# One kernel of attention and two mixtures on one core: another order of the head, value products by 128 rows, another end of the running sums

## The chip, the cores and the metric

The kernel runs on one core of a Trainium2 chip. The metric is the time of one execution on the device in microseconds (us). The engines are TensorE (PE), VectorE (DVE), ScalarE (ACT), GpSimd (POOL) and SyncE (SP), which here only starts transfers. Each works through its own instructions in the order in which the program writes them, and waits where data or a buffer isn't ready. The kernel before takes 391.78 us, the median of three runs.

## The reference, cut to what matters

Three stages follow each other: masked attention over 4 batches of 576 tokens with 8 heads of 64 (heads 0 to 3 see a window of 32 tokens, heads 4 to 7 every 32nd token), a feed-forward block with a squared relu, and a soft mixture of experts with 8 experts of 4 slots.

```python
scores = scale * np.matmul(q, k.transpose(0, 1, 3, 2))
scores = np.where(masks[None], scores, -1e9); scores -= scores.max(-1, keepdims=True)
attn = np.exp(scores); attn /= attn.sum(-1, keepdims=True) + 1e-9
x = (attn @ v).transpose(0, 2, 1, 3).reshape(2304, 512)
...
h = x @ w_in                       # 512 -> 2048
g = np.maximum(h, 0) ** 2
x = g @ w_out                      # 2048 -> 512
...
logits = x @ phi                   # 32 slots
d = np.exp(logits - logits.max(0)); d /= d.sum(0) + 1e-9
slot_input = d.T @ x               # 8 experts x 4 slots
h = np.maximum(slot_input[e] @ w1[e], 0)          # 512 -> 1024
slot_out[e] = h @ w2[e]                           # 1024 -> 512
c = np.exp(logits - logits.max(1, keepdims=True)); c /= c.sum(1, keepdims=True) + 1e-9
out = c @ slot_out
```

## The kernel before, in words

Tokens are cut into five blocks (512, 512, 512, 512, 256). For each block there are 16 product steps, 80 in all: step s multiplies x, transposed, by 128 columns of `w_in` (`gemm1`, L474). x and `w_in` are both kept as a high and a low part, so one step is 12 products. ACT takes the relu out of PSUM (L493), ACT or POOL squares it (L497, L499), and DVE transposes it to tokens (L506). The second matrix is never applied to tokens. `matrix` (L535 to L547) multiplies `w_out` by phi, `logits` (L527) takes the slots' logits from the squared steps, and `Dispatch` keeps a running maximum over tokens (`nm_run`) and running sums: `total` makes logits by slot and the maximum (L569 to L575), `turn` the rescaling factor `al` and the turned weights, and `slots` (L598) is the group-summing product, which sums the squared steps by slot into two PSUM tiles `four`. For blocks 0 to 2 the sums of earlier blocks are kept elsewhere and added; from block 3 on (`KEEP`) `scale` (L590 on ACT, L591 on DVE) rescales `four` in place and `slots` adds to it. In the last block `last_step` (L513 to L515), `last_turn` (L616 to L622) and `last_sums` (L628 copies, L632 products, L633 transposes) do the same, and `hold` (L874) issues dummy products. After that come the slots' inputs (L896 and on), the experts (L935, L962) and the output (L980).

Attention is cut into 16 units, one for each batch and pair of heads; pairs 0 and 1 are local, pairs 2 and 3 strided. For the first eight units PE writes the mask (L247) and the scores (L258), DVE takes the negative row maxima (L262), PE subtracts them (`less`, L268), and ACT takes the exponential (L274). DVE sums (L319) and inverts (L322 to L325), POOL or DVE scales (L328), and PE turns the weights into the PSUM tile `turned` (L342), from which ACT or DVE moves them to `ptl` or `pts` (L353); later units turn on DVE (L363). The value products (L391) write two tiles, `oa` and `ob`. The high part of x is a cast (L406), the low part a subtraction on DVE (L407).

The weights' bits arrive as raw words (L424, SP) and are put together before use: ACT brings the upper word into range (L442), DVE shifts (L445) and joins the lower word (L449); for `w_in` a cast to the high part (L454, on ACT, POOL or DVE) and the low part (L458, on DVE or POOL) follow. Conversions 0 to 7 are `w_in` (tiles `y`), from 8 on the other matrix (tiles `wo`).

What sets the order: everything up to product step 18 stands in a hand-written string `HEAD`, whose tokens are issued one after the other: `A3` is the next step of unit 3, `C2` the next step of conversion 2, `G4` a quarter of product step 4, `R`, `X`, `T` its relu, square and transpose, `P` a step of `matrix`, `L` logits, `q`, `v`, `l`, `f` loads, `w9` nine dummy products (L742). A letter A, D or P at the end names the engine. Later work hangs on positions, four for each step (`at(position, function)`), which run between the quarters of a product step. So an engine's order is that of the tokens that use it.

The functions are printed here with the line numbers that the profile uses.

## Time and profile before

| | |
|---|---|
| median of three runs | 391.78 us (391.52 to 394.02) |
| profiled execution, its own time | 393.14 us |
| its span, first to last instruction | 391.3 us |
| mean granted clock of TensorE | 0.992 |
| busy: PE / DVE / ACT / POOL | 368.7 / 246.1 / 176.7 / 55.5 us |
| HBM read | 75.25 MB, 204 GB/s over the span with what is written |

A row of the timeline gives the start of an instruction (or of several alike in sequence, with their count), its duration, the engine, the line and the tiles, and in brackets the idle time of that engine just before it with what ended that. A product in fp32 leaves two or more records, so counts of records on PE are not counts of products. A row of the stretches gives each engine's busy time between two points of the span, then PE's granted clock as a share of 2.4 GHz, the transfers' share and their rate.

### The profile page before, as it was taken

Reading aid. Unit: us, or ns where it says so; the run is one execution under the profiler, and the core shown is the slowest. Engines: PE = TensorE matmul, PEld = TensorE weight load, DVE = VectorE, ACT = ScalarE, POOL = GpSimd, SP = SyncE. Lnnn points to the kernel's source line nnn. Section 1 sums busy time; section 2 is a strip of 40 time slices with the busy share of each in tenths; the row PEclk is TensorE's granted clock in tenths of the full one; section 3 lists DMA queues with packets and bytes.
Section 4 is the critical chain, followed back from the end, with each engine's and each line's share of the span. In section 5 each row is a group of like instructions: output and inputs, shape, how many; then the busy total and the mean of one; then the engine's idle time right before and its main releaser. Section 6 shows DMA issues by size and latency. Waiting matters only on the chain.

```text
span 391.3 us, 9218 instructions
## 1 busy us (share of the span) xinstructions
PE 368.7 (94%) x3822; PEld 261.7 (67%) x3822; DVE 246.1 (63%) x519; ACT 176.7 (45%) x377; POOL 55.5 (14%) x87
## 2 busy tenths in 40 slices
...
GB/s 243 365 156 396 216 299 309 105 107 243 176 37 92 278 3 75 190 116 123 85 52 78 125 55 219 265 56 162 109 54 151 410 407 381 302 379 411 409 360 239
DMA packets 25353, 80.56 MB, mean 206 GB/s; under 512 B 3040, under 2 KB 3296, under 8 KB 25312
## 3 DMA queue, kind: packets, MB, share of 16 engines
...
q14 instruction: 11, 0.09, 0.1%
HBM read 75.25 MB, written 4.72 MB: 204 GB/s over the span
## 4 chain that ended last, share of the span: by engine, by line
PE 80%; DVE 6%; ACT 3%; issue 2%; DVEq 0%; ACTq 0%
PE h L474 50%; PE four L598 5%; PE so L962 4%; PE eh L935 4%; PE four L527 3%; PE oa L391 3%; PE lg L527 2%; PE out L980 1%; PE ob L391 1%; PE si L896 1%; DVE wo L449 1%; PE lr L569 1%; DVE y L449 1%; PE qa L288 1%; PE pp L535 1%
## 5 line engine op out<-in xcount | busy, mean ns | idle before, releaser
L474 PE MATMUL h<-x,w 128*128 128x512 f32 x768 | 191.6, 400 | 3.2 <-DVE x L407 1.2
L474 PEld LDWEIGHTS h<-x,w 128*128 128x128 f32 x768 | 140.5, 188 | 52.0 <-issue 17.4
L493 ACT ACTIVATE gk<-h 128x512 f32<-128x512 f32 (+1 forms) x70 | 38.4, 550 | 93.8 <-PE h L474 88.0
L506 DVE STREAM_TRANSPOSE gt<-gk 128x512 f32<-128x512 f32 (+1 forms) x71 | 44.4, 641 | 46.5 <-ACT gk L497 40.7
L497 ACT ACTIVATE gk<-gk 128x512 f32<-128x512 f32 (+1 forms) x66 | 38.3, 583 | 1.4
L474 PEld LDWEIGHTS h<-xl,w 128*128 128x128 f32 x192 | 23.6, 191 | 3.5 <-issue 3.4
L474 PE MATMUL h<-xl,w 128*128 128x256 f32 x192 | 25.0, 287 | 0.0
L363 DVE STREAM_TRANSPOSE ptl<-sl 32x320 f32<-32x320 f32 (+1 forms) x48 | 23.7, 493 | 0.7
L449 DVE SCALAR_TENSOR_TENSOR wo<-raw,wo 128x512 uint32<-128x512 uint32 x32 | 23.0, 737 | 0.3
L442 ACT ACTIVATE wo<-raw 128x512 f32<-128x512 f32 x32 | 20.8, 667 | 4.9 <-DMA raw<-woutt 3.6
L598 PE MATMUL four<-gt,lsb 32*32 32x512 f32 x576 | 21.4, 598 | 0.7 <-ACT four L590 0.7
L458 POOL TENSOR_TENSOR w<-y,w 128x512 fp32r<-128x512 f32 x10 | 13.2, 1330 | 34.7 <-ACT w L454 34.7
L598 PEld LDWEIGHTS four<-gt,lsb 32*32 32x32 f32 x576 | 10.0, 103 | 9.2 <-issue 3.5
L407 DVE TENSOR_TENSOR x<-oa,x 128x512 fp32r<-128x512 f32 (+1 forms) x16 | 10.5, 657 | 8.1 <-ACT x L406 5.6
L962 PE MATMUL so<-e,gk 128*32 128x128 f32 (+1 forms) x304 | 14.7, 302 | 0.0
L935 PE MATMUL eh<-e,lsb 128*32 128x512 f32 x104 | 14.3, 594 | 0.4 <-DVE lsb L913 0.4
L406 ACT CAST x<-oa 128x512 fp32r<-128x512 f32 (+1 forms) x16 | 9.6, 598 | 11.0 <-PE oa L391 10.8
L363 DVE STREAM_TRANSPOSE pts<-sw 32x512 f32<-32x512 f32 x20 | 14.0, 700 | 0.6 <-POOL sw L328 0.3
L445 DVE TENSOR_SCALAR wo<-wo 128x1024 uint32<-128x1024 uint32 x16 | 12.4, 777 | 2.3 <-ACT wo L442 2.3
L962 PEld LDWEIGHTS so<-e,gk 128*32 128x32 f32 x304 | 11.1, 110 | 2.4 <-issue 0.8
L799 POOL COPY lsb<-pt 128x128 f32<-128x128 f32 x1 | 0.3, 290 | 85.0 <-PE four L598 85.0
L454 ACT CAST w<-y 128x512 fp32r<-128x512 f32 x15 | 9.1, 617 | 5.7 <-DVE y L449 5.6
...
## 6 DMA issues: line engine op xcount, KB each, us to landing
...
```

Source lines behind the costliest of these rows:

```text
L363: yield "T", lambda e, d=dst, s_=src: DVE.transpose(out=d, in_=s_)
L391: PE.matmul(o[bank][64 * h:64 * h + 64, col:col + w1_ - w0], u.v[0:k, t, 64 * h:64 * h + 64], rhs, start=start, stop=stop, skip_group_chec ...
L442: ACT.activation(y[0][:, z], raws[2 * m + z][:, :, 1].bitcast(F32), AF.Prelu, scale=2.0 ** -112, alpha=2.0 ** 32)
L449: DVE.scalar_tensor_tensor(out=yb, in0=raws[2 * m + z][:, :, 0], scalar=29, in1=yb, op0=ALU.logical_shift_right, op1=ALU.bitwise_or)
L474: PE.matmul(hs[s][0][:, 0:TB[b]], w_in[s % SB][:, a, 128 * kc:128 * kc + 128], x_of(b, kc)[:, x, :] if b < 4 else xl[:, :, kc, x, :], star ...
L493: ACT.activation(gs[s], h[:, 0:TB[s // SB]], AF.Relu)
L497: ACT.activation(gs[s], gs[s], AF.Square)
L506: DVE.transpose(out=by_tokens(b)[:, :, f, :] if b else gt_[0].rearrange("p (f t) -> p f t", f=SB)[:, f], in_=gs[s])
L527: PE.matmul(lg_of(b)[q(y), 0:TB[b]], pt[:, f, :], gs[SB * b + f], start=ch == 0, stop=ch == 3, skip_group_check=True)
L598: PE.matmul(four_[a // 2][q(c % 4), a % 2, :], ext[q(a), c, :], g[q(a), c] if self.b else g[q(a), :, 32 * c:32 * c + 32], start=c < 4 and ...
L935: PE.matmul(hps[g][n][q(j), :], siT[:, kc, :], cols(et[0, g, j, kc], 512 * n, 512), start=kc == 0, stop=kc == 3, skip_group_check=True)
L962: PE.matmul(sums[n][q(j)], hT[g][fc // 4][:, fc % 4, q(j)], cols(et[1 + n, g, j, wd * fc // 1024], wd * fc % 1024, wd), start=g == 0 and f ...
```

## The change

There are three parts. First, `HEAD` is another string of the same 520 steps: the same work in another order, with other engine letters at some steps. On DVE there are fewer moves L353 (5 for 16) and, in exchange, 5 casts L406 and 2 casts L454; on ACT 35 moves L353 for 24, 43 casts L406 for 48 and 5 casts L454 for 15; on POOL 9 casts L454 for 1 (whole program). The nine dummies come first. Second, the last fifth of a local unit's keys (64 of them) is multiplied by all 128 rows of the tiles; the other rows hold zeros. Third, in the last block the running maximum is brought into the maximum's tile by a product with the identity, so that one reduction gives the new one; the running sums are copied to SBUF eight and six positions before the last product step ends, `slots` starts from zero, and eight products with `tal`, the identity times the rescaling factor, add the old sums in `last_sums`.

Of `HEAD`, the first line of each string is shown.

```diff
--- before.py
+++ after.py
@@ -26,6 +26,8 @@
 NSTEP = SB * NBLK
 NG = 7
 NX = 14
+OLD = 1536
+OLD_AT = (8, 6)
 NEG = -1e30
 HEAD_ROW = [0, 1, 0, 1]
 UNITS = [(1, 2), (1, 0), (1, 3), (1, 1), (2, 0), (2, 2), (2, 1), (2, 3), (3, 0), (3, 2), (3, 1), (3, 3)]
@@ -35,22 +37,22 @@
 RAW_AT = [0, 1, 2, 3, 4, 6, 0, 1, 2, 0, 1, 2, 0, 1, 2, 0]
 Y_AT = [2, 0, 0, 1, 1, 3, 3, 2]
 HEAD = """
-A2P A0 A0 A0D w9 q2 A0P A0 A0 A0P A0A A0D A2P A2 A1D w6 A0P l0 C0 l10 l1 C0 C0 C0 A2P A2D A2 A2 A2P C0 f l2 l3 q1 A1P
...
+w9 A0 A0 A0D A0P A0 A0 A0P A0A A2P q2 A2P A2 A0D w6 l2 C1 l3 C1 C1 A2P A2D A2 A2 A0P A0A A0A A0A A0A A0A A0A C1D q1
...
 """
 FILL = 6
 HEAD_STEPS = 18
@@ -65,7 +67,7 @@
 LATE_TZ = 26
 LATE_LZ = 37
 EPS = 1e-9
-HOLD = [5, 1, 0]
+HOLD = [5, 0, 0]
 KEEP = 3
 
 C_ML, C_MS, C_ID, C_TI, C_RM, C_LO, C_END = 0, 128, 146, 274, 402, 403, 404
@@ -128,6 +130,7 @@
         tiny = cp.tile([128, 104], F32, name="tiny")
         ident = c[:, C_ID:C_ID + 128]
         tident = c[:, C_TI:C_TI + 128]
+        tal = cp.tile([128, NS], F32, name="tal")
         xr = {}
 
         def ring(n, z, shape, dt, name):
@@ -375,10 +378,10 @@
                 if self.local:
                     plan = []
                     for t in range(5):
-                        k, x0, x1 = (64, 512, 576) if t == 4 else (128, 128 * t, 128 * t + 160)
+                        x0, x1 = (512, 576) if t == 4 else (128 * t, 128 * t + 160)
                         for bank, y0, y1 in ((0, x0, min(x1, 512)), (1, max(x0, 512), x1)):
                             if y0 < y1:
-                                plan.append((t, k, y0 - x0, y1 - x0, bank, y0 - 512 * bank, t == 3 * bank, t == 3 + bank))
+                                plan.append((t, 128, y0 - x0, y1 - x0, bank, y0 - 512 * bank, t == 3 * bank, t == 3 + bank))
                 else:
                     plan = [(t, 128, 0, 72, t // 4, 72 * (t % 4), True, True) for t in range(8)]
 
@@ -566,12 +569,15 @@
             def total(self):
                 o = self.o = ps("at", f"lr{self.b}")
                 T = self.T
+                if self.b == NBLK - 1:
+                    PE.matmul(o[:, T:T + 1], ident, bm, start=True, stop=True)
                 PE.matmul(o[:, 0:T], tident, lsb[:, 0:T], start=True, stop=self.b < NBLK - 1)
                 if self.b == NBLK - 1:
                     PE.matmul(o[:, 0:T], lsb[:, 384:512], gs[NSTEP - 1], start=False, stop=True)
-                DVE.tensor_reduce(out=bm, in_=o[:, 0:T], op=ALU.max, axis=AX.X, negate=True)
-                DVE.tensor_tensor(out=nm, in0=bm, in1=nm_run, op=ALU.min)
-                if self.b < NBLK - 1:
+                    DVE.tensor_reduce(out=nm, in_=o[:, 0:T + 1], op=ALU.max, axis=AX.X, negate=True)
+                else:
+                    DVE.tensor_reduce(out=bm, in_=o[:, 0:T], op=ALU.max, axis=AX.X, negate=True)
+                    DVE.tensor_tensor(out=nm, in0=bm, in1=nm_run, op=ALU.min)
                     ACT.activation(lg_of(self.b)[:, 0:T], o[:, 0:T], AF.Exp, bias=nm, accum_out=bs)
 
             def turn(self):
@@ -582,6 +588,8 @@
                 DVE.transpose(out=lsb[:, 0:T], in_=lg_of(self.b)[:, 0:T])
                 ACT.activation(al, nm_run, AF.Exp, scale=-1.0, bias=nm)
                 DVE.tensor_copy(nm_run, nm)
+                if self.b == NBLK - 2:
+                    DVE.tensor_scalar_mul(bm, nm, -1.0)
                 if self.b >= KEEP:
                     self.scale()
 
@@ -597,7 +605,7 @@
                     for a in range(4):
                         PE.matmul(four_[a // 2][q(c % 4), a % 2, :], ext[q(a), c, :],
                                   g[q(a), c] if self.b else g[q(a), :, 32 * c:32 * c + 32],
-                                  start=c < 4 and self.b < KEEP, stop=c >= num - 4, skip_group_check=True)
+                                  start=c < 4 and (self.b < KEEP or self.b == NBLK - 1), stop=c >= num - 4, skip_group_check=True)
 
             def sums(self):
                 for n in range(2):
@@ -611,25 +619,32 @@
 
             def last_turn(self):
                 z = [slice(0, 128), slice(128, 256)]
-                e_ = gk_[0][:, 2560:2816]
+                e_ = gk_[0][:, 0:256]
                 for n in range(2):
                     ACT.activation(e_[:, z[n]], self.o[:, z[n]], AF.Exp, bias=nm, accum_out=(bs, bs2)[n])
                     DVE.transpose(out=lsb[:, z[n]], in_=e_[:, z[n]])
                 ACT.activation(al, nm_run, AF.Exp, scale=-1.0, bias=nm)
-                self.scale()
+                DVE.tensor_scalar_mul(tal, tident[:, 0:NS], al)
                 ov = self.o[:, 0:256].rearrange("p (c a i) -> p c a i", a=4, i=32)
                 for a in range(4):
                     DVE.transpose(out=self.cv[q(a)], in_=ov[q(a), :, a, :])
 
-            def last_sums(self, to):
+            def last_sums(self):
                 o = [ps("h", f"accT{x}") for x in range(2)]
+                old = gk_[0][:, OLD:OLD + 2048].rearrange("p (a z) -> p a z", a=4)
+                to = {}
                 for x in range(2):
                     for n, copy in enumerate((ACT.copy, DVE.tensor_copy)):
-                        copy(to[:, x, 2 * n:2 * n + 2], four_[n][:, :, 256 * x:256 * x + 256])
+                        z = 2 * x + n
+                        to[x, n] = (lsb if z == 3 else gk_[0][:, 512 * z:512 * z + 512]).rearrange("p (a i) -> p a i", a=2)
+                        copy(to[x, n], four_[n][:, :, 256 * x:256 * x + 256])
+                for x in range(2):
+                    for a in range(4):
+                        PE.matmul(o[x][q(a), 0:256], tal, old[:, a, 256 * x:256 * x + 256], start=True, stop=False, skip_group_check=True)
                 for x in range(2):
                     hold(HOLD[1 + x])
                     for a in range(4):
-                        PE.matmul(o[x][q(a), 0:256], tident[:, 0:NS], to[:, x, a], start=True, stop=True, skip_group_check=True)
+                        PE.matmul(o[x][q(a), 0:256], tident[:, 0:NS], to[x, a // 2][:, a % 2], start=False, stop=True, skip_group_check=True)
                     DVE.transpose(out=gT[:, 8 * x:8 * x + 8, :].rearrange("p f s -> p (f s)"), in_=o[x][:, 0:256])
 
             def comb(self):
@@ -800,6 +815,9 @@
                                                     pt[:, NF - 1, :].unsqueeze(1).to_broadcast([128, 4, NS])))
         at(4 * NSTEP - 2, logits, NBLK - 1, 3, 3)
         at(4 * NSTEP - 2, d.copy)
+        for n in range(2):
+            at(4 * NSTEP - OLD_AT[n], lambda n=n: (DVE.tensor_copy if n else ACT.copy)(
+                gk_[0][:, OLD + 1024 * n:OLD + 1024 * n + 1024], four_[n].rearrange("p a z -> p (a z)")))
         cs4, cT, co = {}, {}, {}
 
         def weights(n, eng):
@@ -882,7 +900,7 @@
         flat = gk_[0]
         bt = [flat[:, 512 * n:512 * n + 512] for n in range(6)]
         d.slots()
-        d.last_sums(flat[:, 0:2048].rearrange("p (x a i) -> p x a i", x=2, a=4))
+        d.last_sums()
         lgx.close()
         late.append(pool(base, "late", space=PSUM, reuse_waits="tile"))
         siT = lsb[:, 0:128].rearrange("p (a b) -> p a b", a=4)
```

On PE, at the start of the program: the first rows of before. `wide`, `qa` and `qb` are score tiles, `tiny` holds the row maxima, L728 are six tiny dummies, L742 the nine larger ones.

```order
L728 MATMUL turned<-acc 32x1 x6
L247 MATMUL qa_2_146<-c 128x288
L247 MATMUL wide<-c 128x128
L247 MATMUL wide<-c 128x384
L247 MATMUL qb_0_148<-c 128x128
L258 MATMUL wide<-k_90,q_89 32x128 x16
L258 MATMUL qb_0_148<-k_90,q_89 32x128 x2
L742 MATMUL turned<-acc 128x128 x9
L268 MATMUL wide<-tiny,c 128x512
L268 MATMUL qb_0_148<-tiny,c 64x128
```

The same place of after, whose line numbers are some higher (L757 is L742, L250 is L247, L261 is L258, L271 is L268).

```order
L743 MATMUL turned<-acc 32x1 x6
L757 MATMUL turned<-acc 128x128 x9
L250 MATMUL wide<-c 128x128
L250 MATMUL wide<-c 128x384
L250 MATMUL qb_0_156<-c 128x128
L261 MATMUL wide<-k_91,q_90 32x128 x16
L261 MATMUL qb_0_156<-k_91,q_90 32x128 x2
L271 MATMUL wide<-tiny,c 128x512
L271 MATMUL qb_0_156<-tiny,c 64x128
```

The nine dummies moved from between the scores of unit 0 and the subtraction of its maxima to the front; the mask of unit 2 moved behind unit 0.

On DVE, from the scaling of unit 2 to the low part of unit 1's x, in before (`oa_2`, `ob_2` are unit 2's values, `xl` the last 64 tokens).

```order
L328 TENSOR_TENSOR sw_108<-s_107,tiny 128x16x18
L353 COPY ptl<-turned 32x10x32 x3
L407 TENSOR_TENSOR x_448<-oa_2_430,x_448 128x16x16
L407 TENSOR_TENSOR xl<-oa_2_430,xl 128x16x2
L407 TENSOR_TENSOR x_448<-ob_2_431,x_448 128x16x16
L407 TENSOR_TENSOR xl<-ob_2_431,xl 128x16x2
L445 TENSOR_SCALAR y_473<-y_473 128x1024
L449 SCALAR_TENSOR_TENSOR y_473<-raw_467,y_473 128x512
L449 SCALAR_TENSOR_TENSOR y_473<-raw_469,y_473 128x512
L353 COPY pts<-turned 32x8x18 x4
L407 TENSOR_TENSOR x_521<-oa_1_507,x_521 128x512
```

The same place of after.

```order
L326 RECIPROCAL tiny<-tiny 128x16
L328 SCALAR_TENSOR_TENSOR tiny<-tiny,c 128x16
L409 CAST xl<-oa_2_413 128x16x2
L409 CAST x_431<-ob_2_414 128x16x16
L409 CAST xl<-ob_2_414 128x16x2
L410 TENSOR_TENSOR x_431<-oa_2_413,x_431 128x16x16
L410 TENSOR_TENSOR xl<-oa_2_413,xl 128x16x2
L410 TENSOR_TENSOR x_431<-ob_2_414,x_431 128x16x16
L410 TENSOR_TENSOR xl<-ob_2_414,xl 128x16x2
L448 TENSOR_SCALAR y_448<-y_448 128x1024
L410 TENSOR_TENSOR x_495<-oa_1_470,x_495 128x512
L452 SCALAR_TENSOR_TENSOR y_448<-raw_446,y_448 128x512
```

The scaling (L328) and seven moves (L353) left DVE, casts of unit 2's values came, and unit 1's low part stands ahead of the two joins of `y` rather than behind them.

On ACT, around the relu of step 78 near the end, in before (`h` is the product's tile, `gk` the squared steps, `lg` the last block's logits).

```order
L493 ACTIVATE gk<-h_3388 128x256
L497 ACTIVATE gk<-gk 128x256
L493 ACTIVATE gk<-h_3406 128x256
L497 ACTIVATE gk<-gk 128x256
L564 COPY lsb<-lg_3311 128x256
```

The same place of after.

```order
L496 ACTIVATE gk<-h_3390 128x256
L500 ACTIVATE gk<-gk 128x256
L819 COPY gk<-four_912 128x1024
L496 ACTIVATE gk<-h_3408 128x256
L500 ACTIVATE gk<-gk 128x256
L567 COPY lsb<-lg_3313 128x256
```

The copy of half of the running sums (L819) came in ahead of the relu of step 78, whose square the last logits read; the other half stands on DVE.

## Rows read from the trace of the kernel before

**Rows 1.** Stretches: length, busy us (instructions) by engine, granted clock, DMA share, GB/s

```profile
0.00:21.80 21.80, 15.44 (x202) 12.89 (x203) 8.97 (x23) 6.34 (x13) 8.18 (x22) 1.00 0.92 304
21.80:47.36 25.56, 21.17 (x296) 14.80 (x296) 20.69 (x47) 18.46 (x47) 8.01 (x7) 0.93 0.74 256
47.36:132.71 85.35, 80.91 (x712) 55.79 (x713) 73.70 (x143) 46.67 (x95) 15.63 (x13) 1.00 0.53 183
132.71:322.00 189.29, 189.29 (x1782) 138.44 (x1781) 120.01 (x248) 85.75 (x170) 13.90 (x15) 1.00 0.41 143
```

**Rows 2.** Timeline of PE, 3.5 to 24 us: start, duration, instruction, idle before

```profile
3.94 0.61 PE L247 MATMUL qa<-c 128*128 128x288 f32 x1 [2.15 <-DVE c L726]
...
6.57 1.94 PE L258 MATMUL wide<-k,q 128*32 128x128 f32 x32 [1.38 <-issue]
...
8.85 4.14 PE L742 MATMUL turned<-acc 128*128 128x128 f32 x18
12.82 1.02 PE L268 MATMUL wide<-tiny,c 128*128 128x512 f32 x2
...
21.67 1.12 PE L268 MATMUL wide<-tiny,c 128*128 128x512 f32 x2 [1.74 <-DVE tiny L262]
```

**Rows 3.** Timeline of DVE: maxima of unit 0, end of unit 3's x

```profile
9.17 0.27 DVE L262 TENSOR_REDUCE tiny<-qb 64x2 f32<-64x128 f32 x1
...
47.13 0.23 DVE L407 TENSOR_TENSOR xl<-ob,xl 128x32 fp32r<-128x32 f32 x1
```

**Rows 4.** Groups of DVE, 0 to 140 us: instruction, count, busy, mean ns, idle before

```profile
L449 DVE SCALAR_TENSOR_TENSOR wo<-raw,wo 128x512 uint32<-128x512 uint32 x16 | 12.4, 803 | 0.2
L449 DVE SCALAR_TENSOR_TENSOR y<-raw,y 128x512 uint32<-128x512 uint32 x16 | 11.1, 714 | 0.3
...
L458 DVE TENSOR_TENSOR w<-y,w 128x512 fp32r<-128x512 f32 x6 | 4.5, 748 | 0.0
...
L353 DVE COPY pts<-turned 32x144 f32<-32x144 f32 x12 | 3.6, 298 | 2.7 <-ACT pts L353 2.6
...
L353 DVE COPY ptl<-turned 32x320 f32<-32x320 f32 x4 | 1.9, 482 | 0.1
...
L328 DVE TENSOR_TENSOR sl<-sl,tiny 128x640 f32<-128x640 f32 x2 | 1.6, 825 | 0.1
...
L319 DVE TENSOR_REDUCE tiny<-ss 128x16 f32<-128x288 f32 x3 | 1.4, 453 | 2.3 <-ACT ss L274 2.3
```

**Rows 5.** Groups of ACT, 0 to 140 us: the wide cast of a strided unit's x

```profile
L406 ACT CAST x<-oa 128x256 fp32r<-128x256 f32 x4 | 2.5, 615 | 0.6 <-PE oa L391 0.6
```

**Rows 6.** Timeline of DVE and of POOL at 55 us

```profile
55.04 1.78 DVE L449 SCALAR_TENSOR_TENSOR wo<-raw,wo 128x512 uint32<-128x512 uint32 x1
...
54.88 1.39 POOL L458 TENSOR_TENSOR w<-y,w 128x512 fp32r<-128x512 f32 x1 [4.04 <-ACT w L454]
```

**Rows 7.** Timeline of PE: values of a local unit (168 us) and of a strided one

```profile
168.08 0.52 PE L391 MATMUL ob<-ptl,v 128*64 128x32 f32 x8
168.53 0.97 PE L474 MATMUL h<-x,w 128*128 128x512 f32 x3
...
32.51 0.72 PE L391 MATMUL oa<-pts,v 128*64 128x72 f32 x16
```

**Rows 8.** Timeline of the tail, all engines, 330.3 to 341 us

```profile
330.39 0.38 ACT L493 ACTIVATE gk<-h 128x256 f32<-128x256 f32 x1 [0.61 <-PE h L474]
...
333.97 2.32 PE L874 MATMUL hold<-c 128*128 128x256 f32 x10
...
335.85 1.09 ACT L590 ACTIVATE four<-four,st 128x1024 f32<-128x1024 f32 x1
...
336.99 2.56 PE L598 MATMUL four<-gt,lsb 32*32 32x512 f32 x64 [0.69 <-ACT four L590]
...
340.25 1.34 PE L632 MATMUL accT<-gk,c 128*32 128x256 f32 x16
```

**Rows 9.** Stretch of PE alone: us, PE busy, granted clock, DMA share, GB/s

```profile
23.00:26.50 3.50, 3.50 (x75) 0.51 0.19 39
```

More of the change, by code (lines that the diff above doesn't have):

```diff
@@ L53 @@
-R17 A8D A8 P3 A8 A7A A8 A8 A8 A8 X13D L3 R16 v8 A8 A8 A8 A8 T12 A8 A8 T8 T13
+w9 A0 A0 A0D A0P A0 A0 A0P A0A A2P q2 A2P A2 A0D w6 l2 C1 l3 C1 C1 A2P A2D A2 A2 A0P A0A A0A A0A A0A A0A A0A C1D q1
+A1D A1P A1A A1 l1 v0 A0A A0A A2D C1 C1P C1P C1D A1A A1D A1 A2 A2D A2D A1 l0 C0 C0 A2A A2A A2A A2A A2A A2A C0 A1D C1P
+C0 A3 A0A q3 A3 A3 A0 A0A A1A A3D C0 C0A C0P C0P A0A A0 A1A A1A A1D A3D A1A A3D v2 A2A A2D A3A A1A A1A A1A A1A G0 l5
+l4 C2P C2P A3P A3P A2D A2D A2D A2 C0P A2 A3A A2 A2A v1 A1D G0 G1 A3A A3A A3A C2 A1 A1A A1P C2P C2 C2P A1 l6 q4 A4D A4
@@ new lines @@
+G1 C3D A3A A3A A3A A3A l7 C3 A4D A4D A4 v3 H A3A A3 C3 A3 C3P A3 C3 A3 C3 C3P C3P C2 A3 A3 A3 A3 G0 G1 G1 A4A R1 G0 R0
+A5A C3D C2D A4D A4D l9 l10 C5D l11 C5 C5 C5 C5 l8 C4D C4 C4 C4P C4 C4D C4P C5 C5P C5D C5P G3 G3 G3 G3 R3 C2D G4 G4 G4
+G4 q5 l17 A4 A5A A5 A5 l16 C8 C8 l12 C6 R4 C8 C4P C8 l14 l13 C6D C6 C6 G2 G2 A5 A5P A5 A5D A4P C4P G2 G2 C7 l18 A5D
+X4A C6 R2 l15 C7 C7P l19 C9 C9D C9 C7 C9 C8 A4A C7D C9P A4A A5A C7P C6 A4A C7P C7P G5 A6 G5 G5 G5 G6 G6 G6 G6 G7 G7 G7
+q6 A6A A6 l21 f P0 G7 A6D G9 G9 R5 A4D T4 X3D R6 P0 P0 A4A A4A R7 A5 C6D C6P X1D A4A Z v4 A4 A5P A6P A6P A5 X0A P0 C7P
```

21 lines of the change are left out of this document (7 added, 14 removed).

## The prediction

> **What bounds the kernel now.** I read the busy time of each engine by stretches of the span first, because one share for the whole span hides that three different things set the pace [rows 1]. From 132.71 to 322 TensorE (PE) is busy for all of its 189.29 us: there only fewer or shorter products help, and whatever comes earlier in front of it moves the whole rest forward. Before 132.71 PE has holes: 6.36 us of 21.80, 4.39 of 25.56, 4.44 of 85.35. In the last 85 of these VectorE (DVE) works 73.70 us, ScalarE (ACT) 46.67, GpSimd (POOL) 15.63; in the first 21.80 none of the others is half busy, so that stretch is a chain of short steps in which each waits for the one before. The points at which I cut are events: at 21.80 DVE has the row maxima of unit 1, at 47.36 it ends the low part of the x of unit 3 [rows 3], the last of block 0, and at 132.71 the first group-summing product is about to start.
>
> Second I read the timeline of PE in the first stretch [rows 2] beside that of DVE [rows 3]; third the groups of DVE's instructions up to 140 us with their shapes, since letters that hand an instruction from one engine to another are what the new order mostly changes [rows 4, 5]; last the timeline of the tail [rows 8].
>
> **The change part by part.** *The nine dummy products at the start.* They now stand first on PE, in before behind the products of unit 0. DVE has the maxima of unit 0 at 9.17 + 0.27 = 9.44 [rows 3], but the product that takes them off starts at 12.82, because the dummies run from 8.85 on [rows 2]: 12.82 − 9.44 = 3.4 us of stall on the chain. In after they fall where PE waits anyway, 2.15 us for the constants and 1.38 for the first loads [rows 2], 3.5 together against a length of 4.0 (8.85 to 12.82). So 0.4 to 0.5 stays: a gain of about 3.0. Between there and unit 1's maxima DVE has one L449 fewer, 0.7 [rows 4], and the loads of q and k for unit 1 stand four rows earlier on SP's queue; PE waits 1.74 for those maxima at 21.67 [rows 2]. Sum: 3.0 + 0.7 + 0.3 of that wait = **−4.0**; ends −3.3 (unit 1 as long as before) and −4.5.
>
> *DVE from there to the end of block 0's x.* Counted in both orders up to the same instruction: copies of turned tiles 32x320 from 4 to 1 and 32x144 from 8 to 2, low parts L458 from 3 to 1, sums L319 from 3 to 2, scalings L328 from 1 to 2, and in exchange the two wide casts of unit 2's x and their two narrow ones, which ACT did. By the means [rows 4, 5]: −3 × 0.48 − 6 × 0.30 − 2 × 0.75 − 0.45 + 0.83 + 2 × 0.62 + 0.5 (the narrow casts, taken at under half a wide one each) = −2.6; without the L449 above, which comes back here, −1.9 for this stretch. (That DVE takes as long for a cast as ACT isn't shown; copies of the same kind are 0.30 there, twice that is 0.62.) DVE is idle for 25.56 − 20.69 = 4.9 us here [rows 1]; over the head the largest such item is waiting for ACT's copies of the same turned tiles, 2.6 before the 32x144 ones [rows 4]. These copies now come from ACT alone, and the casts that ACT gives up were themselves waited for. I take half of the idle, −2.4. Together **−4.3**; ends −6.7 (all idle goes) and +1 (ACT, with 18.46 of 25.56 busy, gets 11 copies more and becomes late itself).
>
> *DVE from there to 132.71.* In all DVE works only 0.5 us less before the first group-summing product, so what was saved above comes back: 73.70 + 2.1. The idle here is 85.35 − 73.70 = 11.65, 14% [rows 1]. PE has little slack (4.44), but what PE does here is not what DVE waits for. I take off a quarter of the idle, 3.1: −3.1 + 2.1 = **−1.0**; ends +2.0 (no idle goes) and −6.
>
> *POOL gets eight more casts L454 and 4.7 us more work in the head.* The trace shows what that can cost: one L449 took 1.78 us, against a mean of 0.80, while POOL ran a low part beside it [rows 6]; L449 on `wo` means 0.80 against 0.71 on `y`, 16 × 0.09 = 1.4 [rows 4]. L449 on `y`, L445 and L458 are hindered too; as an estimate I take 4 us for all, beside 8.18 + 8.01 + 15.63 of POOL work less its memsets at the start, some 24 [rows 1]. 4.7 more give 4 × 4.7 / 24 = **+0.8**; ends 0 and +8 (below).
>
> The Trainium skill, page "SBUF — State Buffer", section "Who interferes with whom", has a rule that speaks against this part: DVE and GpSimd share one pair of ports, and by "Whoever issues first gets the shared pair for the whole instruction; the other fully blocks" a cast on POOL can hold up a two-input DVE instruction for its whole length. The row of 1.78 us agrees with a block; the mean of 0.80 says that most pass. By the full rule the term would be the rival's instead of +0.8.
>
> *Local units' values by 128 rows.* The last four products of `ob`, eight records, take 168.53 − 168.08 = 0.45 us; strided ones, all of 128 rows and of 72 columns, take 0.72 / 16 = 0.045 a record [rows 7]. By columns, 32 + 32 + 64 + 64 against 72, four products at that rate would take 2.7 × 2 × 0.045 = 0.24, so 0.21 a unit goes at the most if the two of 64 rows cause all of the difference, and nothing if the shape costs nothing. I take 0.2, as no other reason for the difference stands in the rows. The three later local units lie where PE is full, those in the head beside DVE: 3 × 0.2 = **−0.6**; ends 0 and −1.7 (all eight units).
>
> *Tail.* Gone: the scaling of the sums, ACT's 1.09 at 335.85, which the group-summing product at 336.99 waited for with 0.69 of idle time [rows 8]; and the minimum L573 over 128x1, which I take at 0.2 by the smallest DVE row, 0.23 [rows 3]. But the dummies `hold` keep PE from 333.97 on for 2.32, up to about 336.3, so no more than 0.69 can go. Added: two copies of 128x1024. ACT's, put at the scaling's 1.09, goes between the square before and the relu at 330.39, ahead of which ACT was idle for 0.61: 0.48 later, and PE's logits, which wait for that square, with it [rows 8]. DVE's lies beside products. Eight products with the old sums come ahead of those at 340.25; eight of these are sixteen records, 1.34 there, but half of the time PE waited for copies, so +0.2. Sum: +0.4 − 0.69 − 0.2 + 0.2 = **−0.3**; ends +0.8 and −1.3.
>
> The sum is −4.0 − 4.3 − 1.0 + 0.8 − 0.6 − 0.3 = −9.4. The profiled execution took 393.14 us with a span of 391.3, the median of the three runs is 391.78: 393.14 − 9.4 = 383.7 for it, and 391.78 − 9.4 = **382.4** for the median. All of it up to 132.71 holds its worth afterwards, because PE is full to 322 and moves as a block.
>
> **The rivals.** *Only the start counts.* DVE's work up to 132.71 stays the same, so if its idle time after 21.80 is set by loads and by PE, the gain of the second stretch is given back in the third. Then −4.0 − 0.6 − 0.3 + 0.8 and about −1.2 for the 0.5 of work and a little idle: −5.3, **386.5**. For it: 0.5 us is all that the counts give. Against it: the largest idle items of DVE name ACT, and the new order gives just these to other engines.
>
> *Most of the idle goes.* A walk by hand through the waits of the new order with the durations of before ends block 0's x some 9 us earlier and the first group-summing product 10 to 13 earlier; with values and tail that is −14, **378**. Against it: such a walk knows no late loads and no ports.
>
> *POOL's work blocks DVE.* If each of the some nine additional POOL instructions holds a DVE instruction as the longest one was held, 1.78 − 0.80 = 0.98 [rows 4, 6], that is 8.8 in the place of 0.8: −1.4, **390.4**, no change. For it: the casts stand right where L449 runs. Against it: the ten low parts of POOL in before show one such row at this size, not ten.
>
> *TensorE stays at its lower level: slower.* From 23.0 to 26.5 the granted clock is 0.51, that is 1.2 instead of 2.4 GHz, after PE had stood idle for 1.74 ahead of 21.67 [rows 2, 9]. In before the nine dummies kept PE busy without a break from 6.57 to the products of unit 0; in after that bridge is gone and PE waits there for each step of DVE and ACT. Of the 21.17 us that PE works in the second stretch [rows 1] about 19.4 are at the upper level's length (3.5 at half is 1.75). The stretch has 4.39 of PE idle; so each us that falls to the lower level beyond 4.4 lengthens the head, and from 9.4 + 4.4 = 13.8 us on the gain is eaten. All 19.4 would cost 15: **397.4**. [...]
>
> **How the numbers follow.** A measurement of this kernel can tell about 1% from no change, 3.9 us: faster means under 387.9. Chances: the forecast, with its own range 379.5 to 385, 0.50; only the start 0.22; most of the idle 0.12; POOL 0.10; TensorE's level 0.06. Faster: 0.50 + 0.12 and of the 386.5 case, whose own bounds (values 0, POOL +2) reach across 387.9, 0.18: 0.80. No change: 0.10 of POOL, 0.04 of that case less a little that goes further: 0.13. Slower 0.07. The range goes from 376.5 (the wide case with its own error) to 389: below lie some 0.07, above the POOL and the TensorE case with 0.13.
>
> **What would show it.** Right: unit 0's subtraction on PE starts by about 10 us with no dummies between it and the maxima; the end of unit 3's x on DVE near 39; the first group-summing product near 123; from there to step 78 the same length less 0.6; in the tail the wait for the scaling gone and a wait of the logits of the last block for the relu of step 78 of some 0.4 in its place. Wrong: unit 3's x early but the group-summing product near 128 (only the start); L449 at 1.3 us and more in the mean (POOL); granted clock at 0.5 beyond 30 us (level); PE idle behind 330 for over 1.5 us more (tail).

## The result, and the profile after

The kernel after takes 376.73 us, the median of four runs (376.36 to 377.13); beside it the kernel before took 392.9, the median of four. The ratio is 0.959, with a 95% interval of 0.9545 to 0.9633. So it is 16 us faster where 9.4 were forecast; the time lies just inside the range's lower end, below the forecast's own range, and next to the rival "most of the idle goes" (378). The profiled execution took 376.57 us.

First the stretches of after, cut at the same events as in [rows 1]: unit 1's maxima, the end of unit 3's x, the first group-summing product (columns as there; the last cut lies 0.43 us ahead of that product in before and 0.16 behind it in after, so by the events the third stretch is 85.8 and 81.0 us long).

```profile
0.00:17.21 17.21, 14.30 (x202) 11.86 (x203) 7.96 (x22) 6.06 (x13) 7.61 (x21) 1.00 0.92 284
17.21:36.86 19.65, 17.67 (x295) 13.58 (x296) 17.54 (x43) 17.11 (x45) 7.96 (x9) 1.00 1.03 348
36.86:118.00 81.14, 80.11 (x730) 57.00 (x745) 76.00 (x145) 45.41 (x93) 24.30 (x20) 1.00 0.64 214
118.00:310.00 192.00, 192.00 (x1811) 141.74 (x1799) 120.62 (x249) 87.86 (x176) 14.09 (x15) 1.00 0.42 148
```

The first group-summing product, in before and in after:

```profile
133.14 2.42 PE L598 MATMUL four<-gt,lsb 32*32 32x512 f32 x65
```

```profile
117.84 1.76 PE L606 MATMUL four<-gt,lsb 32*32 32x512 f32 x37
```

The events came 4.6 us earlier (21.80 to 17.21), 10.5 (47.36 to 36.86) and 15.3 (the first group-summing product, 133.14 to 117.84); nearly the whole gain is there. DVE's idle time fell from 4.87 to 2.11 us in the second stretch and from 11.65 to 5.1 in the third. PE now stands idle for 1.98 and 1.03 there (4.39 and 4.44 before): with so little left, it has become what bounds the head behind unit 1's maxima too. Its granted clock is 1.00 in the second stretch, 0.93 before.

The start against [rows 2, 3], first PE, then DVE; columns as there.

```profile
1.72 4.21 PE L757 MATMUL turned<-acc 128*128 128x128 f32 x18
...
7.28 1.08 PE L261 MATMUL wide<-k,q 128*32 128x128 f32 x32 [0.71 <-issue]
...
9.16 1.12 PE L271 MATMUL wide<-tiny,c 128*128 128x512 f32 x2 [0.60 <-DVE tiny L265]
...
15.18 1.08 PE L261 MATMUL wide<-k,q 128*32 128x128 f32 x32
...
17.08 1.12 PE L271 MATMUL wide<-tiny,c 128*128 128x512 f32 x2 [0.61 <-DVE tiny L265]
```

```profile
9.02 0.27 DVE L265 TENSOR_REDUCE tiny<-qb 64x2 f32<-64x128 f32 x1
...
36.66 0.20 DVE L410 TENSOR_TENSOR xl<-ob,xl 128x32 fp32r<-128x32 f32 x1
```

The subtraction of unit 0's maxima (L271) starts at 9.16 for 12.82: PE waits 0.60 for the maxima of `wide` and starts without waiting for those of `qb`, which end at 9.29. The scores of unit 0 take 1.08 for 1.94, which is TensorE's upper level (without the dummies they take 1.93, below). Unit 1's scores come at 15.18, and PE waits 0.61 for its maxima where it waited 1.74.

What became of the groups in [rows 4 to 6], 0 to 125 us (columns as in rows 4), DVE and then POOL:

```profile
L452 DVE SCALAR_TENSOR_TENSOR wo<-raw,wo 128x512 uint32<-128x512 uint32 x16 | 11.7, 756 | 0.1
L452 DVE SCALAR_TENSOR_TENSOR y<-raw,y 128x512 uint32<-128x512 uint32 x16 | 10.6, 684 | 0.1
...
L461 DVE TENSOR_TENSOR w<-y,w 128x512 fp32r<-128x512 f32 x5 | 4.6, 952 | 0.0
```

```profile
L461 POOL TENSOR_TENSOR w<-y,w 128x512 fp32r<-128x512 f32 x11 | 15.0, 1374 | 0.7 <-ACT w L457 0.5
L457 POOL CAST w<-y 128x512 fp32r<-128x512 f32 x9 | 8.8, 985 | 31.5 <-DVE y L452 10.6 <-ACT gt L496 6.5 <-issue 6.3
```

In before the one cast on POOL took 604 ns (the same view):

```profile
L454 POOL CAST w<-y 128x512 fp32r<-128x512 f32 x1 | 0.6, 604 | 0.0
```

With 8.7 us more of POOL work in the third stretch DVE's joins (L452) are shorter than before, not longer; its subtractions L461 are longer, 952 ns for 748 [rows 4].

The tail, against [rows 8], and below it the two rows of before that it is measured by:

```profile
313.86 1.00 ACT L819 COPY gk<-four 128x1024 f32<-128x1024 f32 x1
...
314.75 0.39 ACT L496 ACTIVATE gk<-h 128x256 f32<-128x256 f32 x1
...
315.53 0.73 PE L530 MATMUL lg<-gk,pt 128*32 128x256 f32 x6
...
318.24 2.32 PE L892 MATMUL hold<-c 128*128 128x256 f32 x10
...
319.39 0.66 DVE L625 STREAM_TRANSPOSE lsb<-gk 128x128 f32<-128x128 f32 x2 [0.53 <-ACT gk L624]
...
320.49 2.37 PE L606 MATMUL four<-gt,lsb 32*32 32x512 f32 x64
...
324.87 2.37 PE L914 MATMUL si<-wo,pt 128*32 128x256 f32 x40
```

```profile
331.36 0.63 PE L527 MATMUL lg<-gk,pt 128*32 128x256 f32 x6
...
341.54 0.83 PE L896 MATMUL si<-wo,pt 128*32 128x256 f32 x9
```

From the logits to the slots' inputs (L914, L896 of before) it takes 9.34 us for 10.18. The group-summing product (L606) no longer waits for a scaling, but for the last of the dummies `hold`.

### The profile page after: what moved, and what is told of

The parts are those of the page before. It is cut to its first block, busy times and chain, and to the rows that moved or that the text cites. A ratio compares the mean times of both kernels' runs of the same rounds, so it can differ in the third digit from the quotient of the medians.

```text
span 374.5 us, 9255 instructions
## 1 busy us (share of the span) xinstructions
PE 362.0 (97%) x3838; PEld 260.4 (70%) x3838; DVE 243.8 (65%) x516; ACT 173.6 (46%) x373; POOL 63.7 (17%) x95
## 4 chain that ended last, share of the span: by engine, by line
PE 85%; DVE 9%; DMA 2%; ACT 1%; issue 1%; SPq 1%; POOL 0%; DVEq 0%; ACTq 0%; POOLq 0%
PE h L477 49%; PE four L606 6%; PE so L980 4%; PE eh L953 4%; PE oa L394 3%; PE four L530 3%; PE lg L530 2%; DMA ph<-phi 2%; PE turned L757 2%; DVE ptl L366 1%; PE ob L394 1%; PE out L998 1%; DVE wo L452 1%; PE qa L291 1%; PE lr L574 1%
## 5 line engine op out<-in xcount | busy, mean ns | idle before, releaser
L477 PE MATMUL h<-x,w 128*128 128x512 f32 x768 | 188.1, 398 | 0.0
L477 PEld LDWEIGHTS h<-x,w 128*128 128x128 f32 x768 | 141.0, 188 | 45.8 <-issue 15.6
L496 ACT ACTIVATE gk<-h 128x512 f32<-128x512 f32 (+1 forms) x70 | 38.5, 551 | 87.2 <-PE h L477 86.8
L500 ACT ACTIVATE gk<-gk 128x512 f32<-128x512 f32 (+1 forms) x68 | 39.5, 584 | 1.4
L452 DVE SCALAR_TENSOR_TENSOR wo<-raw,wo 128x512 uint32<-128x512 uint32 x32 | 22.3, 715 | 0.2
L606 PE MATMUL four<-gt,lsb 32*32 32x512 f32 x576 | 21.3, 598 | 0.0
L606 PEld LDWEIGHTS four<-gt,lsb 32*32 32x32 f32 x576 | 9.7, 103 | 8.6 <-issue 3.8
L461 POOL TENSOR_TENSOR w<-y,w 128x512 fp32r<-128x512 f32 x11 | 15.0, 1374 | 0.7 <-ACT w L457 0.5
L457 POOL CAST w<-y 128x512 fp32r<-128x512 f32 x9 | 8.8, 985 | 31.5 <-DVE y L452 10.6
L315 POOL TENSOR_TENSOR sl<-sl,tiny 128x640 f32<-128x640 f32 x4 | 5.4, 1340 | 49.4 <-DVE tiny L314 49.4
```

The source lines that it names most:

```text
L452: DVE.scalar_tensor_tensor(out=yb, in0=raws[2 * m + z][:, :, 0], scalar=29, in1=yb, op0=ALU.logical_shift_right, op1=ALU.bitwise_or)
L461: ENG[e].tensor_tensor(out=w[:, 1], in0=y[0][:, z], in1=w[:, 0].bitcast(F32), op=ALU.subtract)
L477: PE.matmul(hs[s][0][:, 0:TB[b]], w_in[s % SB][:, a, 128 * kc:128 * kc + 128], x_of(b, kc)[:, x, :] if b < 4 else xl[:, :, kc, x, :], star ...
L496: ACT.activation(gs[s], h[:, 0:TB[s // SB]], AF.Relu)
L500: ACT.activation(gs[s], gs[s], AF.Square)
L606: PE.matmul(four_[a // 2][q(c % 4), a % 2, :], ext[q(a), c, :], g[q(a), c] if self.b else g[q(a), :, 32 * c:32 * c + 32], start=c < 4 and ...
```

## The experiments

Ratios are to runs of the kernel before on the same chip, whose medians were 394.03, 393.16 and 394.06 for the three sets of four. Those runs spread from 391.6 to 396.6 and those of after over less than 1 us, so runs of the new order are compared with after by their own medians. After itself wasn't run in these sets; beside it stand, on their chips, the kernel that lacks only the new tail (377.26, second set) and the one with a dummy less in the tail (376.97, third set), both within 0.6 us of its 376.73.

**The new order of the head alone.** Everything but the string is as before.

```diff
-A2P A0 A0 A0D w9 q2 A0P A0 A0 A0P A0A A0D A2P A2 A1D w6 A0P l0 C0 l10 l1 C0 C0 C0 A2P A2D A2 A2 A2P C0 f l2 l3 q1 A1P
...
+w9 A0 A0 A0D A0P A0 A0 A0P A0A A2P q2 A2P A2 A0D w6 l2 C1 l3 C1 C1 A2P A2D A2 A2 A0P A0A A0A A0A A0A A0A A0A C1D q1
...
```

> The kernel before with the new order of the head alone; values and tail as before. After came out 16.2 us under before where 9.4 were forecast. Theory A (the head was undersized): the first group-summing product starts near 117.8 as in after and the time is 377.5 to 378.5, ratio 0.962 to 0.965. Theory B (the tail or the values gave more than forecast, the trace of after only shifts it): 380 to 384, ratio 0.970 to 0.980.

Measured: 378.42 us (378.25 to 378.45, and 381.53 for the profiled execution, in which the clock was granted at 0.95 throughout; so its events aren't compared). Ratio 0.9624, 0.9581 to 0.9668. The head is 15.6 of some 17 us in this set (394.03 against after's 376.73): theory A. Values and tail share the 1.7 us that are left to after.

**The order and the letters apart.** First the new order with each step on the engine that it had before, second the old order with the engines of after; 60 letters differ. One line of each, against the string with the same order:

```diff
-w9 A0 A0 A0D A0P A0 A0 A0P A0A A2P q2 A2P A2 A0D w6 l2 C1 l3 C1 C1 A2P A2D A2 A2 A0P A0A A0A A0A A0A A0A A0A C1D q1
+w9 A0 A0 A0D A0P A0 A0 A0P A0A A2P q2 A2P A2 A0D w6 l2 C1 l3 C1 C1 A2P A2D A2 A2 A0P A0A A0A A0A A0A A0A A0D C1D q1
...
-A1A A1 A1A C1 C1 C1 C1D C0P A0A A0A A0A A0A A0A A0D C1 A1D A1 A1 A3 q3 A3 A3 A0A A0A A2 A2A A2D C0 A2A A2A A2A A2A C0D
+A1A A1 A1A C1 C1 C1 C1D C0A A0A A0A A0A A0A A0A A0A C1 A1D A1 A1 A3 q3 A3 A3 A0A A0A A2 A2D A2D C0P A2A A2A A2A A2A
...
```

> The kernel before with the steps in the new order, but every step on the engine that it had before (60 letters differ). My forecast counted the relief of VectorE by the letters as a term of its own (2.6 us up to the x of unit 3). Theory W (work of VectorE): the order alone gives what is left of some 15, 10 to 12 us, ratio 0.970 to 0.975. Theory I (idle times: steps stand where their inputs come): nearly all, 13 to 15 us, ratio 0.962 to 0.967. Rival: letters and order only fit together, and the order with the old letters gives under 6 us, ratio over 0.985.

> The kernel before with the old order of the steps, but each step on the engine that it has in after. Theory W: 2 to 4 us less, ratio 0.990 to 0.995. Theory I: within 1 us of before. Rival (fit together): slower than before by 2 us and more, ratio over 1.005, since steps handed to ScalarE and GpSimd stand behind others there.

Measured: the order alone 401.44 us, ratio 1.0177 (1.014 to 1.0214); the letters alone 407.84, ratio 1.0364 (1.0331 to 1.0397). Both are slower than before; together they gain 15.6. The rival of both runs is right and my two theories are wrong: neither order nor letters gain anything by themselves. The longest waits of PE in the head (engine, line, releaser: us, times, longest), for the order alone and then for the letters alone:

```profile
PE h L474 <- ACT gt L493: 5.4, 2, 4.8
PE oa L391 <- issue: 3.6, 3, 1.3
```

```profile
PE turned L342 <- DVE sw L328: 5.8, 1, 5.8
```

The last row shows one place where it goes wrong: unit 4's scaling, on POOL in before (at 49.87), stands with the new letter on DVE, but in the old order behind five joins there, and starts at 63.51; PE waits 5.8 us, up to 64.42, to turn its result. (The new letters move the scalings of units 2 and 4 from POOL to DVE and that of unit 3 the other way.)

**The dummies at the front in the old order, then unit 1's loads earlier besides, then a bridge.** Three steps on one string:

```diff
-A2P A0 A0 A0D w9 q2 A0P A0 A0 A0P A0A A0D A2P A2 A1D w6 A0P l0 C0 l10 l1 C0 C0 C0 A2P A2D A2 A2 A2P C0 f l2 l3 q1 A1P
+w9 A2P A0 A0 A0D q2 A0P A0 A0 A0P A0A A0D A2P A2 A1D w6 A0P l0 C0 l10 l1 C0 C0 C0 A2P A2D A2 A2 A2P C0 f l2 l3 q1 A1P
...
-w9 A2P A0 A0 A0D q2 A0P A0 A0 A0P A0A A0D A2P A2 A1D w6 A0P l0 C0 l10 l1 C0 C0 C0 A2P A2D A2 A2 A2P C0 f l2 l3 q1 A1P
+w9 A2P A0 A0 A0D q2 A0P A0 A0 A0P A0A A0D A2P A2 A1D w6 A0P l0 C0 l10 q1 l1 C0 C0 C0 A2P A2D A2 A2 A2P C0 f l2 l3 A1P
...
+w9 A1A A1 A1A C1 C1 C1 C1D C0P A0A A0A A0A A0A A0A A0D C1 A1D A1 A1 A3 q3 A3 A3 A0A A0A A2 A2A A2D C0 A2A A2A A2A A2A
```

> The kernel before with the nine dummy products moved to the front of the program, nothing else. By the forecast's first term the subtraction of unit 0's maxima starts 3.0 us earlier (9.8 for 12.8) and the whole ends 2.5 to 3 us earlier, ratio 0.992 to 0.994. Rival (given back): the time is caught by loads or by ScalarE before unit 1's maxima and the end moves by under 1 us. Rival (TensorE's level): the products of unit 0 run at 1.2 GHz and the end is no earlier or later than before.

Measured: 393.7 us, ratio 1.0001 (0.9972 to 1.003). The timeline of PE shows both rivals at once, the one of TensorE's level at unit 1 rather than unit 0:

```profile
9.19 1.13 PE L268 MATMUL wide<-tiny,c 128*128 128x512 f32 x2 [0.61 <-DVE tiny L262]
...
18.90 1.93 PE L258 MATMUL wide<-k,q 128*32 128x128 f32 x32 [3.72 <-DMA k<-kd]
...
21.64 2.08 PE L268 MATMUL wide<-tiny,c 128*128 128x512 f32 x2 [0.39 <-DVE tiny L262]
```

Unit 0 is 3.6 us earlier, where 3.0 were worked out. But unit 1's scores wait 3.72 us for k and start at 18.90, for 18.64 before, and behind that hole every product takes about twice as long (2.08 for 1.12): the granted clock is 0.50 from 20 to 25 us and 0.66 from 25 to 30.

> The kernel before with the nine dummies at the front, and besides the loads of unit 1's q and k issued behind two weight loads rather than six other transfers. In the run with the dummies alone the scores of unit 1 waited 3.72 us for k and started at 18.90 (18.64 before), so nothing came through. Theory L (the dummies and the load were each enough to hold unit 1): its scores start near 15 to 16, its maxima 2.5 to 3.5 us earlier than before, and some of that, 1 to 4 us, reaches the end: ratio 0.990 to 0.997. Rival (DVE's order caught it): scores early, but the end within 1 us of before.

Measured: 392.73, ratio 0.9997 (0.9972 to 1.0021). Unit 1's maxima end at 18.40, 3.4 us earlier, and the end doesn't move: the rival's result. Whether for its reason, DVE's order, isn't shown: PE now waits 2.44 us for those maxima, and the granted clock is 0.53 from 20 to 25 us.

> The run before this in the old order (dummies at the front, unit 1 loaded earlier) and nine more dummy products between the scores of unit 1 and the subtraction of its maxima, where TensorE had stood idle for 2.44 us. In that run unit 1 came 3.4 us earlier, but the granted clock was 0.53 from 20 to 25 us and 0.79 from 25 to 30, and nothing of it reached the end. Theory C (the level gave it back): the clock stays at 1.00 up to 30 us, the x of unit 3 ends at 43.5 to 45.5 (46.83 there, 47.36 before), and the whole is 1.5 to 3.5 us under before, ratio 0.991 to 0.996. Rival (VectorE's order gave it back): clock at 1.00, but x of unit 3 after 46 and the end within 1 us of before.

Measured: 395.42, ratio 1.0043 (1.0015 to 1.0071). The clock stays at 1.00 up to 40 us (then 0.66 for 5 us), so the bridge did what it should, and yet unit 3's x ends at 47.09 (46.83 without the bridge, 47.36 before). Theory C's forecast falls. The waits of ACT in this run, 18 to 48 us, and rows of its timeline:

```profile
ACT y L442 <- DMA raw<-win: 3.2, 2, 1.7
```

```profile
20.00 0.66 ACT L442 ACTIVATE y<-raw 128x512 f32<-128x512 f32 x1 [1.72 <-DMA raw<-win]
20.68 2.15 ACT L353 COPY ptl<-turned 32x320 f32<-32x320 f32 x5
22.74 0.58 ACT L274 ACTIVATE sl<-wide 128x512 f32<-128x512 f32 x1
```

The same three steps in after:

```profile
15.00 3.35 ACT L356 COPY ptl<-turned 32x320 f32<-32x320 f32 x8 [0.84 <-PE turned L345]
18.38 0.60 ACT L277 ACTIVATE sl<-wide 128x512 f32<-128x512 f32 x1
...
19.03 1.26 ACT L445 ACTIVATE y<-raw 128x512 f32<-128x512 f32 x2
```

ACT now waits 3.2 us for raw words of `w_in`; in before it waits for none there. The last of them come with a load issued at about 10.2, behind unit 1's, that lands 9.8 us later. Behind that conversion ACT has, in the old order, the moves of unit 0's turned tile and then unit 1's exponential: they start at 20.68 and 22.74, for 20.32 and 22.83 in before, although unit 1's subtraction on PE comes 2.0 us earlier (19.65 for 21.67). So what the start won ends on ACT. In the new order the moves and the exponential stand ahead of these conversions, which then wait for nothing. That this is what the old order lacked is read from the traces; it wasn't tried alone. Nor is the level quite out of it: at 33.90 ACT is still 1.2 us earlier than in before (35.11), and behind the stretch at 0.66 only 0.27 is left at the end of unit 3's x.

**The dummies back, in the new order; and none.** The first puts `w9` behind unit 0's first maximum, the second leaves the nine out (they compute nothing).

```diff
-w9 A0 A0 A0D A0P A0 A0 A0P A0A A2P q2 A2P A2 A0D w6 l2 C1 l3 C1 C1 A2P A2D A2 A2 A0P A0A A0A A0A A0A A0A A0A C1D q1
+A0 A0 A0D w9 A0P A0 A0 A0P A0A A2P q2 A2P A2 A0D w6 l2 C1 l3 C1 C1 A2P A2D A2 A2 A0P A0A A0A A0A A0A A0A A0A C1D q1
...
-w9 A0 A0 A0D A0P A0 A0 A0P A0A A2P q2 A2P A2 A0D w6 l2 C1 l3 C1 C1 A2P A2D A2 A2 A0P A0A A0A A0A A0A A0A A0A C1D q1
+A0 A0 A0D A0P A0 A0 A0P A0A A2P q2 A2P A2 A0D w6 l2 C1 l3 C1 C1 A2P A2D A2 A2 A0P A0A A0A A0A A0A A0A A0A C1D q1 A1D
...
```

> The kernel after with the nine dummies back between the maxima of unit 0 and their subtraction. Theory L: unit 0 holds the start again, the first group-summing product comes 3 to 3.6 us later and the time is 379.5 to 381, which is 3 to 4 us over after (376.7), ratio about 0.966 to 0.970. Rival (slack after the start swallows it, as in before): within 1 us of after, ratio 0.957 to 0.961.

Measured: 380.24 (379.79 to 380.46), ratio 0.9672 (0.9641 to 0.9703): 3.5 us over after, as theory L has it, and the first group-summing product at 121.5 for 117.8. In the new order the place of the dummies is worth somewhat more than the first term's 3.0; in the old one nothing.

> The kernel after without its nine dummy products at the front. My slower rival said that without a bridge TensorE stays at 1.2 GHz; here it has none at all up to the mask of unit 0. Theory C: the scores of unit 0 run at the lower level, as in before (1.94 us for 1.08), the subtraction of its maxima comes 0.5 to 1 us later, and then the clock is up or stays low for some stretch: 1 to 5 us over after, ratio 0.961 to 0.971. Rival (the waits for loads cover it): within 0.6 us of after, ratio 0.957 to 0.960.

Measured: 379.53 (378.21 to 380.5), ratio 0.963 (0.9595 to 0.9666), 2.8 us over after, as theory C has it. PE without the nine:

```profile
7.04 1.93 PE L261 MATMUL wide<-k,q 128*32 128x128 f32 x32 [2.09 <-issue]
...
9.77 2.08 PE L271 MATMUL wide<-tiny,c 128*128 128x512 f32 x2 [0.39 <-DVE tiny L265]
...
14.05 2.23 PE L757 MATMUL turned<-acc 128*128 128x128 f32 x12
16.11 0.65 PE L271 MATMUL qa<-tiny,c 128*128 128x288 f32 x2
```

The products up to 14 us run at half the rate (1.93 for 1.08, 2.08 for 1.12), the twelve dummies at 14.05 take 2.23 for 1.60, and from 16 us on the rate is the full one; unit 1's subtraction comes at 20.03 for 17.08. Useless products in time that is idle anyway are worth almost 3 us here.

**GpSimd's casts.** In the new order the nine casts go to ScalarE; in the old order the sixteen casts go to the engines of after. The diff shows one line of each; each string is wrapped anew.

```diff
-C0 A3 A0A q3 A3 A3 A0 A0A A1A A3D C0 C0A C0P C0P A0A A0 A1A A1A A1D A3D A1A A3D v2 A2A A2D A3A A1A A1A A1A A1A G0 l5
+A3 A0A q3 A3 A3 A0 A0A A1A A3D C0 C0A C0 C0P A0A A0 A1A A1A A1D A3D A1A A3D v2 A2A A2D A3A A1A A1A A1A A1A G0 l5 l4
...
-A1A A1 A1A C1 C1 C1 C1D C0P A0A A0A A0A A0A A0A A0D C1 A1D A1 A1 A3 q3 A3 A3 A0A A0A A2 A2A A2D C0 A2A A2A A2A A2A C0D
+A1A A1 A1A C1 C1 C1 C1D C0A A0A A0A A0A A0A A0A A0D C1 A1D A1 A1 A3 q3 A3 A3 A0A A0A A2 A2A A2D C0P A2A A2A A2A A2A
...
```

> The kernel after with its nine casts L457 on GpSimd handed to ScalarE, as nearly all were in before. Theory P (port: GpSimd blocks VectorE, the term of +0.8): the joins L452 on wo fall from 756 ns to under 720 and the time falls by up to 1 us. Theory S (GpSimd was the one that is held, its casts take 985 ns beside 604 alone, and ScalarE has no room at these places): slower than after by 2 to 8 us, ratio 0.965 to 0.980, with VectorE waiting for ScalarE's casts and copies.

Measured: 386.02 (383.8 to 386.64), ratio 0.9811 (0.9771 to 0.985): 9.3 us over after, theory S and beyond its upper end of 8. The joins on `wo`, and PE's waits up to 130 us:

```profile
L452 DVE SCALAR_TENSOR_TENSOR wo<-raw,wo 128x512 uint32<-128x512 uint32 x16 | 10.7, 695 | 0.1
```

```profile
PE h L477 <- ACT gt L496: 3.3, 1, 3.3
PE turned L345 <- POOL sw L331: 1.7, 1, 1.7
PE turned L345 <- ACT pts L356: 1.5, 1, 1.5
```

The joins on `wo` are 756 − 695 = 61 ns shorter, 1.0 us for sixteen, as theory P has it for the port; that is small beside what ScalarE's lateness costs. It delays unit 3's x by 4.4 us (41.30 for 36.86) and stretches the way from there to the first group-summing product to 86.8 us, as long as in before (85.8). It also adds holes on PE, and the clock falls to 0.70 from 30 to 35 us and 0.69 from 60 to 70; what part of the 9.3 us that is was not separated.

> The kernel before in its own order, but the sixteen casts to the high part stand on the engines of after: 9 on GpSimd, 5 on ScalarE, 2 on VectorE (1, 15 and none before). In the new order, nine of them back on ScalarE cost 9.3 us. Theory S (ScalarE's relief is worth it anywhere): faster than before by 2 to 6 us, ratio 0.985 to 0.995. Rival (only where the order leaves the cast time to wait): slower by 2 to 8 us, ratio 1.005 to 1.02, as a cast of 1 us and a queue on GpSimd stand ahead of the low part.

Measured: 394.77, ratio 1.0036 (1.0008 to 1.0063): slower by 0.7 us by the medians and by 1.4 by the ratio, under the rival's lower figure but on its side. These casts too pay only in the order that was made for them.

**Values and tail.**

```diff
-                        k, x0, x1 = (64, 512, 576) if t == 4 else (128, 128 * t, 128 * t + 160)
+                        k, x0, x1 = (128, 512, 576) if t == 4 else (128, 128 * t, 128 * t + 160)
```

> The kernel before with the new order of the head and the values by 128 rows, without the new tail. New order alone took 378.4, after 376.7. By the forecast's terms the values are worth 0.6 and the tail 0.3; the sum is 1.7. Theory T (the tail is what was undersized, as the two traces say: 1.0 from the relu of step 78 on): 377.6 to 378.0. Rival (values undersized): 376.9 to 377.3.

Measured: 377.26 (376.87 to 377.66), ratio 0.9598 (0.9572 to 0.9624). So by the medians the values are worth 1.2 us and the tail 0.5, which is the rival's figure (values undersized). But the runs with and without the values stand on two chips, the intervals of all three ratios overlap, and the traces say otherwise: from the first group-summing product to the slots' inputs it is 207.95 us here and 207.03 in after, 0.9 for the tail, and from that product to the relu of step 78 it is 196.81 here and 197.25 in before, 0.4 for the values behind the head. Where the rest of the 1.2 would be isn't shown. The value products in after:

```profile
152.74 0.40 PE L394 MATMUL ob<-ptl,v 128*64 128x32 f32 x8
153.07 1.19 PE L477 MATMUL h<-x,w 128*128 128x512 f32 x4
```

That is 0.33 for 0.45 [rows 7], 0.12 a unit, which for three units is the 0.4 just named.

```diff
-HOLD = [5, 0, 0]
+HOLD = [4, 0, 0]
```

> The kernel after with four dummy products instead of five in the tail. In after the turned weights are ready at 320.05 us, but the group-summing product starts at 320.49, when the fifth dummy ends. Theory: 0.3 to 0.45 us under after, 376.3 to 376.45, the product directly behind the fourth dummy. Rival (the level falls in the gap, or the product waits for something else): within 0.15 us of after or slower.

Measured: 376.97 (375.95 to 377.3), ratio 0.9563 (0.9536 to 0.9589). In the trace the group-summing product follows 1.82 us behind the first `hold` (2.25 in after), directly as the weights are ready: 0.43 gained at that place. In the whole time it can't be told from after, which is the rival's result.

## Why the prediction came out as it did

The direction and the mechanism, a head that waits less, are right; the size is some 7 us short. By the traces the terms are −4.6, −5.9, −4.8, −0.4 and −0.9, together −16.6, the difference of the two profiled executions; the term of POOL has no place of its own in that sum. The time lies 0.2 us inside the range, and that is luck: the range reaches down there only by the wide end of "most of the idle goes", which had a chance of 0.12, and the forecast's own range ended at 379.5.

**The start, −4.0.** The trace gives −4.6, and the size of "a gain of about 3.0" for the dummies holds in the new order (3.5). What failed is that it stood as a term of its own: in the old order the same edit gives nothing, first because k of unit 1 comes no earlier, and with k earlier and the clock held because ACT, by the trace, then waits for the next weights' raw words. "A gain of about 3.0" was read from the first wait alone and carried to the end without asking which load, copy or clock is late next.

**To the end of unit 3's x, −4.3.** It was −5.9: DVE worked 3.15 us less (1.9 forecast) and stood idle 2.76 less (2.4). Overlooked was a row that I had read and used only for the rival on TensorE's level: 3.5 us at 0.51 [rows 9] are 1.75 us of lost PE work in before, and after has no such stretch. The rival had the sign wrong: in this stretch the new order leaves PE 1.98 us of holes for 4.39, and the level stays up.

**From there to the first group-summing product, −1.0.** This is the step that failed: it was −4.8 by the events and −4.2 by the stretches. DVE's work came back as counted (+2.3, forecast 2.1), but "I take off a quarter of the idle" (which is 2.9, not 3.1) should have been over half: −6.5 of 11.65. The reason given, that PE isn't what DVE waits for, was true and beside the point: DVE waited for ACT. Its longest waits for ACT in this stretch (engine, line, releaser: us, times, longest), in before and then in after:

```profile
DVE x L407 <- ACT x L406: 2.4, 2, 1.3
DVE wo L445 <- ACT wo L442: 2.3, 3, 1.4
DVE tiny L319 <- ACT ss L274: 1.7, 1, 1.7
DVE y L445 <- ACT y L442: 1.1, 2, 0.6
```

```profile
DVE c_all L587 <- ACT four L581: 0.9, 1, 0.9
DVE wo L448 <- ACT wo L445: 0.5, 1, 0.5
DVE x L410 <- ACT x L409: 0.2, 1, 0.2
```

These are 7.5 us in before and 1.6 in after, and that is nearly all of the 6.5. ACT lost ten casts L454; with nine of them back on ACT the stretch is as long as in before (86.8 us by the events) and the first group-summing product comes at 128.1 rather than 117.8.

**POOL, +0.8.** Wrong in sign as a statement on the casts. What DVE pays for them is there (1.0 us by the run with the casts on ACT), but the same casts on ACT cost 9.3; I had priced what POOL does to DVE and not what ACT's relief does to all that queues on ACT. The work was undercounted too: POOL has 39.87 us up to the end of the third stretch for 31.82, 8.0 more and not 4.7. The port rival (+8.8) falls all the same. The Trainium skill, page "SBUF — State Buffer", section "Who interferes with whom", says who issues first decides who is held. One row of after fits it: a cast on POOL that starts within a train of five DVE joins (56.09 to 59.17) ends only behind them.

```profile
56.89 2.76 POOL L457 CAST w<-y 128x512 fp32r<-128x512 f32 x1 [6.48 <-ACT gt L496]
```

By this one the nine casts take 985 ns in the mean (median 679), against 604 for the single one of before, 3.4 us in all. DVE is held as well, its five subtractions L461 by some 1.0 us (952 ns for 748), while its joins are no longer than before. So here it is mostly POOL that is held, and POOL has the time.

**Values −0.6, tail −0.3.** By the traces −0.4 (three units of 0.12) and −0.9. In the tail the feared 0.4 us behind the copy of the old sums didn't come: the relu of step 78 starts 196.91 us after the first group-summing product, and 196.81 in the run without the copy, so it is 0.1 late, and PE has no idle time before the logits that follow.

**The rivals.** "Most of the idle goes" came nearest, and its argument, a walk through the waits of the new order, was the better method: it put unit 3's x at some 9 us earlier (10.5) and the first group-summing product at 10 to 13 (15.3), short of both. I had preferred halves and quarters of idle time. "Only the start counts" falls, as its own start gives nothing alone.
